# Retention and FFN on one core: the tails' block moved ahead of the last batch, FFN units regrouped so that w_out loads in long runs

## The chip, the cores and the metric

The kernel runs on one core of a Trainium2 chip. A core has a matrix engine (TensorE, PE in the profile, with its weight loads as PEld), VectorE (DVE), ScalarE (ACT), GpSimd (POOL) and SyncE (SP), which here only issues transfers. Data come from HBM into SBUF (128 partitions) through 16 DMA engines; matmul results go to PSUM, in banks of 128 x 512 fp32. The metric is the device time of one execution in microseconds. The kernel before takes 301.15 us, the median of 3 runs (301.05 to 301.19).

## The reference

Eight batches of 576 positions, eight heads of 64. Scores get a decay per head and a causal mask, there is no softmax; the result of all heads, side by side, is the input of an FFN with an ELU.

```python
scores = scale * np.matmul(q, k.transpose(0, 1, 3, 2))
Dmat = np.where(rel >= 0, gamma[:, None, None] ** rel[None, :, :], 0.0)
ret = scores * Dmat[None, :, :, :]
attn_out = np.matmul(ret, v)                      # [8, 8, 576, 64]
x = attn_out.transpose(0, 2, 1, 3).reshape(4608, 512)
h = x @ w_in                                      # w_in  [512, 2048]
g = np.where(h > 0.0, h, np.exp(np.minimum(h, 0.0)) - 1.0)
out = g @ w_out                                   # w_out [2048, 512], out [4608, 512] fp32
```

The order of the 2048 hidden units does not matter for the result, as long as the columns of w_in and the rows of w_out are taken in the same order.

## The kernel before

**Attention.** The 576 positions of a batch are two stretches of 256 and a tail of 64. An "item" is one stretch of one batch for four heads: q, k and v are loaded by SP, scaled by the decay factors into `qkn` (mostly on GpSimd), transposed (`qkT`; on TensorE for the first seven items, `turn_pe`, by a DMA transposition later), and matmuls then form scores, a state per 64 positions and the output. The tails of four batches make one item each, `t0` and `t1`; they come last in `ORDER`, and their operands lie in the tile `aside`. `put_x` copies the results into `xt`, the transposed FFN input.

**FFN.** Rows go in blocks. Blocks 0 to 5 are narrow (256 rows of the first three batches); 6, 8, 10, 12 and 14 are wide (512 rows of batches 3 to 7); "T" is wide too and holds the 512 tail rows. `ffn1` makes, for 128 hidden units (`ft`) at a time, four accumulating matmuls with weights from `w_in_sb` and `xt` moving; then ACT takes the exponential (L1145), ACT or VectorE the maximum with 0 (L1153, L1155), VectorE subtracts 1 and takes the minimum into `g` (L1160). For a wide block one unit fills a PSUM bank, for a narrow block two do. `ffn2` makes 128 output rows: 16 accumulating matmuls with `g` as weights and `w_out_sb[:, ft]` moving, then a copy to `ot` (L1200) and a store by SP (L1208). `rows_of` says which rows a tile of 128 stores: one transfer of 128 rows for batch rows, two of 64 for tails and for the tiles named in `HALVED`. The last 128 rows of all are cut by columns at `LAST`, 256, 128 and 128.

**Weights.** `w_in_sb` is [128, 4, 2048] and `w_out_sb` [128, 16, 512], both bf16; GpSimd's queue loads and converts them, four transfers each (L471, L479), issued between 9.2 and 20.1 us. The partition p of `w_out_sb[:, ft]` has to hold the row of w_out for the hidden unit that FFN1 left in partition p of the unit group `ft`.

**Order.** Nothing is ordered by hand. Every step is an `Op` with costs per engine, dependencies and a rank; `Plan.run` plays them through and gives each engine a fixed order, which is kept in the program. `seq` is the order of the FFN blocks, "T" put in `TAILS` places from its end; `base` and the ranks follow from it. DMA transfers have assumed durations, for w_out `dma=(2.62, 32, PIECE)`, which the change leaves alone. SP issues in its fixed order too, so that a store which waits for its copy holds up the loads and transpositions behind it.

**The places that matter below.** Item 4 is the first whose loads wait (`HOLD`, a small GpSimd memset at 20.66 us) until w_in is on its way; its q, k and v are issued at 20.82, 21.23 and 21.78 us, while w_in and w_out are still moving. Its q and k are scaled on GpSimd (L494) and transposed on TensorE (L558). At the end of the program stand the last copies and stores of the last FFN2 tile.

Of the kernel before, what the change touches and what calls it, by code (L numbers as in the profile page):

```python
# [17 lines left out]
P = 128  # L18
# [18 lines left out]
class Plan:  # L37
# [6 lines left out]
    def add(self, *a, **kw):  # L44
        op = Op(*a, **kw)
        self.ops.append(op)
        for key in op.use:
            self.users.setdefault(key, []).append(op)
            op.turn += self.owner.get(key, [])
        for cls, key, *_ in op.take:  # L50
            self.owner[key] = [op]
            if cls not in FREE and key not in LONE:
                op.turn += self.takers.get(cls, [])
                self.takers[cls] = [op]
        return op
# [147 lines left out]
TOGETHER = 1  # L203
EARLY = 5
LOOSE = True
TAILS = 0
NARROW = 3
SPREAD = 0
POOL0 = 3.6
# [9 lines left out]
AWAY = {}  # L219
TWO = False  # L220
LAST = (0, 256, 384, 512)
HALVED = ((12, 1),)
ORDER = (0, 1, 2, 3, 4, 5, 6, 7, "t0", "t1")
PE_TURN = 7
WG = ("ck11", "ck11", "ck11", "ck12")
# [16 lines left out]
def kernel(  # L242
# [18 lines left out]
    KJ = DM // P  # L261
# [13 lines left out]
    def mm(*a, **kw):  # L275
        return pin(nc.tensor.matmul(*a, **kw))  # L276
# [66 lines left out]
    w_in_sb = const.tile([P, KJ, DF], BF16, name="w_in_sb")  # L343
# [10 lines left out]
    def T(cls, key, shape, dt):  # L354
        return (cls, key, shape, dt)
# [20 lines left out]
    seq = [*range(2 * NARROW), *range(2 * NARROW, 2 * B, 2)]  # L376
    seq.insert(len(seq) - TAILS, "T")
    place = {blk: i for i, blk in enumerate(seq)}
# [6 lines left out]
    def xt_of(blk):  # L385
        return "xt", blk if blk == "T" else blk // 2
# [90 lines left out]
    def load_w_out(n, after):  # L477
        def emit(op):
            pin(nc.gpsimd.dma_start(w_out_sb[:, 4 * n : 4 * n + 4],  # L479
                                    moe_w_out[n * 512 : (n + 1) * 512, :].rearrange("(f p) n -> p f n", p=P)))  # L480

        w_out_ld[n] = add(f"wo{n}", {"POOL": 0.8}, [], emit, -1000, dma=(2.62, 32, PIECE), after=after)

# [479 lines left out]
    def by_block(key):  # L963
        return tiles[key].rearrange("p k n -> p (k n)").rearrange("p (t k n) -> p t k n", k=KJ, n=P)
# [156 lines left out]
    def ffn1(blk, p, rank):  # L1121
        hkey, ekey, gkey = ("h", blk, p), ("e", blk, p), ("g", blk, p)
        wide, xkey = width[blk] > TB, xt_of(blk)
        at0 = 0 if wide else blk % 2 * TB

        def emit(op):
            ph, xt = tiles[hkey], tiles[xkey]
            for f in range(1 if wide else 2):
                ft = p if wide else 2 * p + f
                for j in range(KJ):  # L1130
                    if blk == "T":
                        o, x = ph, xt[:, j]
                    else:
                        x = by_block(xkey)[:, at0 // P : (2 * TB if wide else at0 + TB) // P, j]
                        o = ph if wide else ph[:, f * TB : (f + 1) * TB]
                        o = o.rearrange("p (t n) -> p t n", n=P)
                    mm(o, w_in_sb[:, j, ft * P : (ft + 1) * P], x, start=(j == 0), stop=(j == KJ - 1))

        f1 = add(f"F1_{blk}_{p}", {"PE": 0.864 if wide else 0.873}, [*xdone[blk], w_in_ld[p // 4 if wide else p // 2]],
                 emit, rank, take=[T("f", hkey, [P, 512], FP32)], use=[xkey],  # L1140
                 after=None if LOOSE and place[blk] < 2 else chain.get(1))
        chain[1] = f1

        def emit_e(op):
            pin(nc.scalar.activation(tiles[ekey], tiles[hkey], AF.Exp))  # L1145

        ex = add(f"ex_{blk}_{p}", {"ACT": 0.6}, [f1], emit_e, rank, take=[T("e", ekey, [P, 512], FP32)],
                 use=[hkey], banks=[(hkey, 0)])

        def emit_m(op):  # L1150
            ph = tiles[hkey]
            if op.eng == "ACT":
                pin(nc.scalar.activation(ph, ph, AF.Relu))  # L1153
            else:
                pin(nc.vector.tensor_scalar_max(ph, ph, 0.0))  # L1155

        md = add(f"md_{blk}_{p}", {"ACT": 0.6, "DVE": 0.66}, [ex], emit_m, rank, use=[hkey], banks=[(hkey, 0)])

        def emit_g(op):
            pin(nc.vector.scalar_tensor_tensor(tiles[gkey], tiles[ekey], -1.0, tiles[hkey], ALU.add, ALU.min))  # L1160

        gdone[blk, p] = add(f"g_{blk}_{p}", {"DVE": 0.69}, [md], emit_g, rank, take=[T("g", gkey, [P, 512], BF16)],
                            use=[hkey, ekey], banks=[(hkey, 0)])

    def rows_of(blk, it):
        if blk == "T":
            return [(j * ST, ST, (2 * it + j) * S + FT * P) for j in range(2)]
        row = blk // 2 * S + blk % 2 * TB + it * P
        if (blk, it) in HALVED:
            return [(0, ST, row), (ST, ST, row + ST)]  # L1170
# [161 lines left out]
    for op in order:  # L1332
# [8 lines left out]
        if op.eng == "PE":  # L1341
            gap = op.start - last if op.start < 50 and op.take else 0.0
            if gap > 0:
                spot = tiles[op.take[0][1]]
                for n in range(int(gap * 0.8 / (0.107 if op.start < 7.0 else 0.056))):
                    if op.name.startswith("T"):
                        pin(nc.tensor.transpose(spot[:, n % 4], zero[:, :P], ident))
                    else:
                        mm((spot if len(spot.shape) == 2 else spot[:, 0])[:, :P], zero[:, :P], zero[:, :P],
                           start=True, stop=True)  # L1350
# [35 lines left out]
```

## Time and profile before

| | |
|---|---|
| median of 3 runs | 301.15 us (301.05 to 301.19) |
| the profiled execution | 300.55 us, of which the span from first to last instruction 298.8 us |
| TensorE's first matmul of the FFN / last matmul of all | 18.3 us / 294.0 us |
| weight loads of w_in / of g | 768 / 608, mean 98 ns each |
| narrow FFN1 matmuls (128 x 256) / wide (128 x 512) | 384 / 384 |
| FFN2 matmuls, 512 / 256 / 128 columns | 560 / 16 / 32 |
| issue to landing, median: w_in, w_out (512 KB each) | 9.2 us, 16.2 us |
| longest waits of TensorE by the profile | 1.3 us (start), 0.4 us, 0.3 us, 0.2 us |
| last matmul to end of span | 4.8 us |

A matmul's duration in the profile overlaps the next one's, since they are pipelined; the pace is read from the distance of starts. In the tables of groups a line gives engine, operation, output and inputs by name, shapes and the count, then busy time and the mean duration. In a timeline the first two numbers are start and duration in us, and the bracket at the end names what the engine waited for and how long. DMA lines name a queue: q0 is GpSimd's, q1 is SP's. A queue's share counts the time of its packets, and packets overlap, so that it can pass 100%.

### The profile page before, as it was taken

What the parts mean: (1) busy time and instruction counts of PE and PEld (TensorE: products, weight loads), DVE (VectorE), ACT (ScalarE), POOL (GpSimd) and SP (SyncE); (2) the same over time, 40 slices, a digit from 0 to 9 for tenths busy, and PEclk for the clock granted to TensorE, in tenths of its full rate; (3) what the DMA queues carried; (4) which work ended last, traced back from release to release, by engine and by line L of the source; (5) the groups of instructions that cost most, each with busy time, mean ns of one, the idle gap of its engine ahead of it and who ended that gap; (6) DMA issues with size and microseconds to landing.
All of it is one profiled execution on the core that took longest, in us unless ns stands there. A gap on an engine that the chain in (4) does not pass through costs nothing.

```text
span 298.8 us, 8957 instructions
## 1 busy us (share of the span) xinstructions
PE 291.7 (98%) x3589; PEld 166.1 (56%) x3589; DVE 175.2 (59%) x315; ACT 199.4 (67%) x391; POOL 136.3 (46%) x257
## 2 busy tenths in 40 slices
PE   7999999999999999999999999999999999999993
PEld 4788656767676754554545454545454544444443
DVE  5989935937765848788656465748353543343200
ACT  2459725858867758769787777787767677767421
POOL 5970379956767655758435546555223000000000
PEclk9999999999999999999999999999999999999999
DMA  7999998998899999999998999976694010110033
GB/s 208 271 207 213 222 289 199 197 194 184 181 204 209 175 217 206 205 182 230 255 249 234 204 176 241 189 168 147 151 162 122 29 37 35 52 56 36 35 72 70
DMA packets 141978, 50.14 MB, mean 168 GB/s; under 512 B 120688, under 2 KB 137456, under 8 KB 141936
## 3 DMA queue, kind: packets, MB, share of 16 engines
q1 hardware_dynamic: 137712, 45.37, 71.5%
q0 software_dynamic: 4224, 4.19, 8.4%
q8 instruction: 28, 0.46, 0.7%
q14 instruction: 14, 0.11, 0.1%
HBM read 36.70 MB, written 9.44 MB: 154 GB/s over the span
## 4 chain that ended last, share of the span: by engine, by line
PE 90%; DMA 3%; DVE 2%; POOL 2%; SPq 0%; issue 0%; ACT 0%; ACTq 0%; DVEq 0%
PE f L276 88%; PE sc L276 2%; DMA rv<-in_v_dram 2%; DMA qkT<-qkn 2%; POOL qkn L494 1%; DVE pt L937 1%; PE f L558 1%; POOL w_in_sb L471 0%; DVE qkn L494 0%; SPq L422 0%; DVE s_mid L834 0%; POOL s_mid L820 0%; POOL vn L545 0%; POOL s_end L820 0%; DVE end L812 0%
## 5 line engine op out<-in xcount | busy, mean ns | idle before, releaser
L1160 DVE SCALAR_TENSOR_TENSOR g<-e,f 128x512 bf16<-128x512 f32 x144 | 96.7, 685 | 86.4 <-ACT f L1153 70.9
L276 PE MATMUL f<-w_out_sb,g 128*128 128x512 bf16 (+2 forms) x608 | 143.3, 368 | 0.0
L276 PE MATMUL f<-xt,w_in_sb 128*128 128x256 bf16 (+1 forms) x768 | 140.9, 326 | 0.0
L1145 ACT ACTIVATE e<-f 128x512 f32<-128x512 f32 x144 | 84.9, 598 | 39.9 <-PE f L276 32.5
L276 PEld LDWEIGHTS <-w_in_sb 128*128 128x128 bf16 x768 | 74.5, 98 | 53.0
L276 PEld LDWEIGHTS <-g 128*128 128x128 bf16 x608 | 56.7, 98 | 58.3
L1153 ACT ACTIVATE f<-f 128x512 f32<-128x512 f32 x123 | 72.6, 592 | 0.0
L494 POOL TENSOR_TENSOR qkn<-rqk,far_q 128x256 bf16<-128x256 f32 x48 | 28.9, 616 | 9.3 <-DMA rqk<-in_q_dram 8.8
L494 POOL TENSOR_TENSOR qkn<-rqk,far_k 128x256 bf16<-128x256 f32 x48 | 29.1, 618 | 8.1 <-DMA rqk<-in_k_dram 7.6
L545 POOL CAST vn<-rv 128x512 bf16<-128x512 f32 x28 | 17.1, 612 | 21.6 <-DMA rv<-in_v_dram 18.8
L1200 ACT COPY ot<-f 128x512 f32<-128x512 f32 (+2 forms) x30 | 16.8, 561 | 11.1 <-PE f L276 11.0
L877 POOL CAST y<-mid 64x256 bf16<-64x256 f32 x36 | 14.2, 400 | 20.4 <-DVE mid L862 9.2
L972 ACT CAST xt<-f 128x512 bf16<-128x512 f32 x23 | 12.4, 589 | 15.9 <-PE f L276 15.9
L931 DVE TENSOR_TENSOR pt<-sc,mask_t 128x1024 bf16<-128x1024 f32 x12 | 14.6, 1218 | 2.4 <-PE sc L276 2.4
L1155 DVE TENSOR_SCALAR f<-f 128x512 f32<-128x512 f32 x21 | 14.6, 693 | 0.9 <-ACT e L1145 0.7
L618 POOL TENSOR_TENSOR aside<-aside,gq 128x256 bf16<-128x256 f32 x16 | 9.4, 615 | 11.6 <-DMA aside<-in_k_dram 11.4
L877 ACT CAST y<-mid 64x256 bf16<-64x256 f32 x31 | 11.9, 401 | 2.3 <-DVE mid L860 1.0
L494 POOL TENSOR_TENSOR qkn<-rqk,gq 128x256 bf16<-128x256 f32 x13 | 8.1, 633 | 11.5 <-DMA rqk<-in_q_dram 11.5
L862 DVE TENSOR_TENSOR mid<-f,mid 128x256 f32<-128x256 f32 x24 | 10.2, 424 | 2.7 <-PE f L276 0.5
L276 PE MATMUL f<-pt,vn 64*64 64x64 bf16 (+1 forms) x512 | 11.6, 202 | 0.1
L993 ACT CAST xt<-f 128x256 bf16<-128x256 f32 x10 | 4.2, 451 | 10.8 <-PE f L276 10.8
L937 DVE TENSOR_TENSOR pt<-sc,mask 128x1024 bf16<-128x1024 f32 x8 | 9.8, 1221 | 2.3 <-PE sc L276 2.2
(93 smaller groups left out, 173.8 us busy)
## 6 DMA issues: line engine op xcount, KB each, us to landing
rqk<-in_q_dram SPq DMA_DIRECT2D x48, 128.0 KB, 3.5
rqk<-in_k_dram SPq DMA_DIRECT2D x48, 128.0 KB, 3.3
rv<-in_v_dram SPq DMA_DIRECT2D x48, 128.0 KB, 3.7
out_dram<-ot SPq DMA_DIRECT2D x23, 256.0 KB, 2.8
rqk<-in_q_dram SPq DMA_DIRECT2D x8, 256.0 KB, 5.8
rqk<-in_k_dram SPq DMA_DIRECT2D x8, 256.0 KB, 5.4
rv<-in_v_dram SPq DMA_DIRECT2D x8, 256.0 KB, 5.6
w_in_sb<-in_moe_w_in_dram POOLq DMA_DIRECT2D x4, 512.0 KB, 9.2
```

What stands on the lines that cost most here:

```text
L276: return pin(nc.tensor.matmul(*a, **kw))
L494: pin(alu[op.eng].tensor_tensor(dst, tiles[raw][:, :, e], g, ALU.mult))
L545: pin(copy[op.eng](tiles["vn", n], tiles["rv", n]))
L877: pin(copy[op.eng](dst, tiles[key][j * D : (j + 1) * D]))
L931: pin(nc.vector.tensor_tensor(tiles[it.pt].rearrange("p i h n -> p (i h n)")[:, : 2 * w * C].rearrange("p (i x n) -> p i x n", i=2, n=C), ...
L937: pin(nc.vector.tensor_tensor(tiles["pt", n].rearrange("p i h n -> p (i h) n"), tiles[it.sc].rearrange("p i (h n) -> p (i h) n", h=2), mas ...
L972: pin(copy[op.eng](by_block(it.xt)[:, 2 * it.T + c], tiles[xkey, c].rearrange("p (h n) -> p h n", n=P)))
L1145: pin(nc.scalar.activation(tiles[ekey], tiles[hkey], AF.Exp))
L1153: pin(nc.scalar.activation(ph, ph, AF.Relu))
L1155: pin(nc.vector.tensor_scalar_max(ph, ph, 0.0))
L1160: pin(nc.vector.scalar_tensor_tensor(tiles[gkey], tiles[ekey], -1.0, tiles[hkey], ALU.add, ALU.min))
L1200: pin(copy[op.eng](tiles[okey][:, :cols], tiles[pkey][:, :cols]))
```

## The change

Three things are changed. (1) The tails' block moves from the last place of `seq` to the last but one, so that block 14 (batch 7) is computed last. (2) Instead of one tile, five tiles are stored in two halves: the last of block 10 and all four of block 12. (3) Of each 512 rows of w_out, partition p now holds rows 4p to 4p + 3 (one run of 2048 numbers in HBM and in SBUF) instead of rows p, 128 + p, 256 + p and 384 + p (four runs of 512). To match, the 128 hidden units of group `ft` become every fourth one of their 512, so FFN1's weight loads read every fourth column of `w_in_sb`, 8 bytes apart, where they read 128 neighbours. The number of instructions on TensorE, GpSimd, ACT and VectorE together stays; SP issues two transfers more.

```diff
-TAILS = 0
+TAILS = 1
...
-HALVED = ((12, 1),)
+HALVED = ((10, 3), (12, 0), (12, 1), (12, 2), (12, 3))
...
-                                    moe_w_out[n * 512 : (n + 1) * 512, :].rearrange("(f p) n -> p f n", p=P)))
+                                    moe_w_out[n * 512 : (n + 1) * 512, :].rearrange("(p f) n -> p f n", p=P)))
...
-                    mm(o, w_in_sb[:, j, ft * P : (ft + 1) * P], x, start=(j == 0), stop=(j == KJ - 1))
+                    mm(o, w_in_sb[:, j, ft // 4 * 512 + ft % 4 : (ft // 4 + 1) * 512 : 4], x, start=(j == 0), stop=(j == KJ - 1))
```

In the built program TensorE's order is the same for its first 5610 of 7180 instructions, which is up to the attention stretch that runs at 201.3 us before. Later the two differ in the order of the blocks. Before, the FFN1 groups of block 14 alternate with FFN2 groups of block 12, those of T with FFN2 of 14, and FFN2 of T stands alone at the end. After, FFN2 of block 12 runs in one piece around the tails' attention, then come the sixteen FFN1 groups of T in one piece, then FFN1 of 14 alternates with FFN2 of T, and FFN2 of 14 stands alone at the end.

## The prediction

> **What bounds the kernel now.** I read the busy table first, then the chain of waits, then the timeline of TensorE, because the first only says who is busy.
>
> ```profile
> span 298.8 us, 8957 instructions
> PE 291.7 (98%) x3589; PEld 166.1 (56%) x3589; DVE 175.2 (59%) x315; ACT 199.4 (67%) x391; POOL 136.3 (46%) x257
> PE 90%; DMA 3%; DVE 2%; POOL 2%; SPq 0%; issue 0%; ACT 0%; ACTq 0%; DVEq 0%
> 20.93 10.65 PE L276 MATMUL f<-xt,w_in_sb 128*128 128x256 bf16 x96
> 31.42 0.39 PE L558 MATMUL f<-ident,qkn 128*128 128x128 bf16 x4
> ```
>
> The last two lines (TensorE timeline, start and duration in us) are 96 FFN1 matmuls of a narrow block from 20.93 to 31.42: 10.49 / 96 = 109 ns each, with no wait between. Wide ones take 16 in 3.45 us (the output copies at 287.22 and 290.68 stand one tile of 16 apart), 216 ns each. FFN1 and FFN2 at these paces are 384 x 0.109 + (384 + 560) x 0.216 + 16 x 0.109 + 32 x 0.056 = 249 us of the 277 us from 17.2 to 294.2 (0.056: the last two 128-column tiles, whose copies start 0.89 us apart for 16 matmuls). Attention is the rest. So TensorE is the bound from 17 us on, its order is fixed in the program, and the change leaves it no matmul fewer. What can move the time: a new wait on TensorE, weight loads that no longer hide, and the 4.6 us behind its last matmul.
>
> **The change part by part: w_out.** Each of four loads copies 512 rows. The diff turns four runs of 512 numbers per partition into one of 2048 (the built copy has the form 128x2048 for 128x4x512). Here is what the DMA queues did from 20 to 24 us (first line) and from 25 to 36 us (the two others): packets, MB written, share of 16 engines.
>
> ```profile
> q0 software_dynamic: 829, 0.82, 123.8%
> ...
> q0 software_dynamic: 1589, 1.58, 84.3%
> q1 hardware_dynamic: 1593, 0.79, 35.5%
> ```
>
> q0 carries w_in and w_out, q1 everything that SP issues. Alone, q0 moved a packet of 1 KB every 4000 / 829 = 4.83 ns. Beside q1 the two alternate, 1589 packets against 1593, a pair every 11000 / 1589 = 6.92 ns, though q1's hold half the bytes. So a q1 packet costs 2.09 ns, and the share goes by packets. The loads of q, k and v for item 4 (SP, from 20.82 us) sit in that stretch: 256 KB in packets of 512 B, 512 packets each, 512 x 6.92 = 3.5 us a load, from about 24.4 us.
>
> If a run of 2048 numbers becomes one packet, w_out is 512 packets of 4 KB. No row has such a pair. At q0's own rate per byte it takes 4 x 4.83 + 2.09 = 21.4 ns, and the first q1 load of 512 packets needs 11.0 us where it needed 3.5: its landing moves by 7.4 us. Bounds: if 4 KB went at the 292 GB/s that both queues reach together from 36 to 40 us, 14.0 + 2.1 = 16.1 ns a pair, 8.3 us, 4.7 us later; by the instruction queue's row (28 packets, 0.46 MB, 0.7% of 16 engines: 1.2 us for 16.4 KB, so 0.6 us for the 8 KB read here, over 16 engines 37 ns) 39.5 ns, 20.2 us, 16.7 us later. I take 7.4, the row with the same bytes and the same cast. Who waits:
>
> ```profile
> 29.23 1.19 POOL L494 TENSOR_TENSOR qkn<-rqk,gq 128x256 bf16<-128x256 f32 x2 [8.43 <-DMA rqk<-in_q_dram]
> 31.31 0.32 PEld L558 LDWEIGHTS <-qkn 128*128 128x128 bf16 x4
> ...
> 32.85 1.19 POOL L494 TENSOR_TENSOR qkn<-rqk,gk 128x256 bf16<-128x256 f32 x2 [2.44 <-DMA rqk<-in_k_dram]
> ```
>
> POOL waits for item 4's q, scales it until 30.42, and TensorE transposes it at 31.42 (second transposition, k's: 34.68). The cover is 31.42 - 30.42 less some 0.1 to hand over, 0.9 us. The wait is then 7.4 - 0.9 = 6.5 us (bounds 3.8 and 15.8). Everything behind it on TensorE stands still, and it is not regained: POOL is in order too, item 4's state blocks stand ahead of item 5, so its busy stretch from 40 to 58 us shifts along. When q is through, w_out is through as well, and k and v follow at q1's own pace, inside the 3.3 us that TensorE takes from one transposition to the next. w_out itself lands earlier, for nothing: its first matmul at 33.4 us waits for no load now.
>
> By the Trainium skill (TensorE: Matmul & The Clock Gate, section Part 1) an idle stretch of some 3.4 us lets the matmul clock fall to half. The trace has the two paces, 423 ns for a 128x512 matmul in the first 4 us against 216 later, but no idle stretch after that to test it. By the page up to 2 us would come on top; the sum below leaves it out.
>
> **FFN1's columns.** 768 weight loads read every fourth column. None in the trace is strided. Contiguous ones take 98 ns each and keep up with a 56 ns pace in the last tiles, so a load has at least a factor of two before a narrow matmul's 109 ns shows it, four before a wide one's 216. Lower bound 0; upper, if four times 56 ns: 384 x (223 - 109) + 384 x (223 - 216) = 46 us. I take 0: the nearest row is the same load with the same bytes.
> By the Trainium skill (SBUF — State Buffer, the note on cachelines) a stride is free while two reads fall in a line of 16 bytes; 8 bytes between columns is just that, so by the page also 0. No run here shows it.
>
> **Tails' block before the last.** TensorE's instructions are the same up to some 200 us, then the same work in another order: the last 128-row tile is now whole rows of a batch, with one store where a tails' tile has two.
>
> ```profile
> 294.25 0.27 ACT L1200 COPY ot<-f 128x128 f32<-128x128 f32 x1 [0.63 <-PE f L276]
> 295.30 1.18 SPq L1208 DMA_DIRECT2D out_dram<-ot  x2
> out_dram<-ot SPq DMA_DIRECT2D x2, 64.0 KB, 2.0
> out_dram<-ot SPq DMA_DIRECT2D x4, 32.0 KB, 1.9
> ```
>
> The last copy ends at 294.52, but its two stores leave SP at 295.30 and 295.89, since four of some 0.6 us queue there. With one store a piece SP is free at 294.52, so the last leaves some 1.3 us earlier and lands in 2.0 us for 1.9. I take -1.3; bounds -0.6 (one issue less) and -1.8 (also the queue ahead of it).
> The price in front: sixteen wide FFN1 units of the tails now run back to back, 13.8 us. ACT then has 16 exponentials and about 10 relus at 0.49 us (two start 0.49 apart where it is full), 12.7 us; VectorE 16 products and 6 relus at 0.64, 14.1 us; six PSUM banks cover the 0.3. The run from 20.93 above was such a burst, and no matmul waited. Before it, the tails' two copies into xt (0.68 us, from 237.11 to 237.79) are covered by one FFN2 group, 0.86 us: 0 to 0.2, I take 0.1.
> The halved stores add issues on SP. Two pairs now stand before the last two transpositions of the tails, one waits for a copy at about 227 us; those transpositions then go at 228.5 and 229.8 instead of 225.1 and 226.5 and land 2.8 later, 232.6, for scores at 234.3. Cover 1.7 us, price 0.
>
> **Sum.** The profiled run took 300.55 us, 298.8 of it the span. 300.55 + 6.5 + 0.1 - 1.3 + 0 = 305.85. The median of the runs is 301.15, 0.6 more: 306.5.
>
> **Rivals.**
> (a) Faster: the software queue cuts the long runs, or the engines share otherwise, so q1 keeps its share and the wait at 31.42 never comes. It decides when q of item 4 lands less than 0.9 us later than now. Then only the end counts: 301.15 + 0.1 - 1.3 = 300.0. For it: all 4096 data packets of q0 have 1 KB, none shows that a longer one exists in that queue. Against it: the instruction queue has packets of 16 KB, the stores 2 KB, so the engines take what they are given.
> The Trainium skill (DMA: Bandwidth & Descriptors, section SWDGE vs HWDGE vs iDMA) lets a packet hold several descriptors up to about 4096 bytes; by that four short runs already went together and the share would not change, which is this rival. The trace's one-for-one alternation of 1 KB pieces differs.
> (b) Strided weight loads become the bound of the narrow blocks: it decides from 109 ns a load. At twice 56 ns, 112, they cost 384 x 3 ns = 1.1 us, at four times 46 us: with (a) 301 to 346. Against it: the hidden room above.
> (c) The long packets go but cut only in two (2 KB): the pair is 11.8 ns, q lands 2.5 us later and k 5.0, less its cover of 0.6: 4.4 us of wait, 304.4. It belongs to the forecast's side.
>
> **How the numbers follow.** Forecast with (c) 0.56, (a) 0.35, (b) 0.09. A measurement of this kernel tells about 0.2%, 0.6 us. Faster: (a) nearly whole, 0.35. Same: 0.03, a small wait and the shorter end cancelling. Slower: the forecast and (b), 0.62. The range reaches to (a) on one side, 300.0 less 0.5 = 299.5, and on the other to 309.5, a wait of 9.5 us, since the upper bound comes from another kind of transfer; left out are most of (b) and the top of the wait, some 0.12. The forecast's own range is 303.8 to 309.5.
>
> **What would show it.** Right: the DMA view shows some 512 packets above 2 KB on q0 and few q1 packets until 35 us; POOL's first scaling of item 4 starts near 36.7; TensorE has one wait of 4 to 8 us, before the transposition after the 96 narrow matmuls; narrow matmuls stay at 109 ns, and the last store leaves SP within 0.1 us of the last copy. Wrong: that scaling still at 29 to 30 us and no wait there, narrow matmuls above 110 ns, or a wait in the tails' burst.

## The result, and the profile after

The changed kernel takes 307.80 us, the median of 4 runs (307.59 to 308.30), where the kernel before takes 301.10 us (300.89 to 301.19). The ratio is 1.0226, 95% interval 1.0208 to 1.0244: slower by 6.7 us. The profiled execution took 308.30 us, 7.75 us more than that of before.

From the page of the changed kernel, its span, the busy table and the shares of the chain of waits:

```profile
span 306.6 us, 8945 instructions
...
PE 295.1 (96%) x3589; PEld 178.2 (58%) x3589; DVE 179.2 (58%) x323; ACT 195.3 (64%) x383; POOL 134.8 (44%) x257
...
PE 91%; DMA 4%; DVE 2%; POOL 1%; issue 0%; ACT 0%; POOLq 0%; ACTq 0%; DVEq 0%
```

TensorE still bounds the kernel, with the same 3589 matmuls. Its share fell from 98 to 96%, so there is a new wait, and its busy time grew by 3.4 us with no matmul more, so some matmuls became slower. TensorE's waits on the changed kernel (engine, line, what it waited for; us in total, times, longest) and its timeline from 18.5 us (start and duration in us; the wait before it in brackets):

```profile
PE f L276 <- DMA w_in_sb<-in_moe_w_in_dram: 6.8, 1, 6.8
PE f L276 <- DVE zero L281: 1.3, 1, 1.3
PE f L558 <- POOL qkn L494: 0.2, 1, 0.2
```

```profile
18.66 0.30 PE L276 MATMUL f<-xt,w_in_sb 128*128 128x256 bf16 x1
25.74 3.37 PE L276 MATMUL f<-xt,w_in_sb 128*128 128x256 bf16 x15 [6.78 <-DMA w_in_sb<-in_moe_w_in_dram]
...
30.35 10.99 PE L276 MATMUL f<-xt,w_in_sb 128*128 128x256 bf16 x96
41.18 0.39 PE L558 MATMUL f<-ident,qkn 128*128 128x128 bf16 x4
```

There is one long wait, but not where the prediction put it. It stands between the first and the second matmul of the whole FFN, and it is for w_in, not for item 4's q. Before, the same 16 matmuls ran without a break:

```profile
18.33 1.92 PE L276 MATMUL f<-xt,w_in_sb 128*128 128x256 bf16 x16
```

The transposition that was to wait (41.18) follows its 96 matmuls at once; it is 9.8 us late only because everything ahead of it is.

The windows of the wait, of the stretch after it and of the next ten microseconds on the changed kernel (stretch, length, then busy time and count of PE, PEld, DVE, ACT, POOL, then the granted clock, DMA share, GB/s):

```profile
18.70:25.70 7.00, 0.25 (x5) 0.06 (x1) 1.76 (x4) 0.00 (x0) 1.67 (x4) 0.65 1.20 212
25.70:31.00 5.30, 5.26 (x42) 3.82 (x43) 1.24 (x3) 2.62 (x5) 0.00 (x0) 0.50 1.06 217
31.00:41.00 10.00, 10.00 (x93) 9.98 (x92) 8.79 (x20) 9.05 (x20) 2.92 (x5) 1.00 1.05 270
```

After the idle 7 us TensorE works for 5.3 us at a granted clock of 0.50: the narrow FFN1 matmuls there start 213 ns apart, where 109 ns is their pace. From 31 us it is whole again. The 0.65 of the first row is a mean: the clock was whole until 20.8 us and 0.50 from there on, so it fell within the wait.

GpSimd's timeline on the changed kernel, and its DMA queues from 24 to 36 us (packets, MB, share of 16 engines):

```profile
36.03 1.19 POOL L494 TENSOR_TENSOR qkn<-rqk,gq 128x256 bf16<-128x256 f32 x2 [14.99 <-DMA rqk<-in_q_dram]
37.36 1.19 POOL L494 TENSOR_TENSOR qkn<-rqk,gk 128x256 bf16<-128x256 f32 x2
```

```profile
DMA packets 2167, 2.79 MB, mean 232 GB/s; under 512 B 107, under 2 KB 1691, under 8 KB 2165
...
q0 software_dynamic: 562, 1.96, 81.1%
q1 hardware_dynamic: 1603, 0.80, 25.4%
```

So w_out does go in long packets. While both queues had work, from 27 to 33 us, they moved 309 and 306 packets, one for one; most of q1's 1603 came after 33 us, when w_out was nearly through. In the whole run q0 has 2688 packets instead of 4224, 1536 fewer, which is 2048 packets of 1 KB become 512 of 4 KB. Item 4's q is scaled at 36.03 instead of 29.23 us, 6.8 us late, where 7.4 was forecast. But TensorE comes for it only at 41.18.

The end, from ACT's and SP's timeline and the list of DMA issues (KB each, median us to landing) of the changed kernel:

```profile
302.38 2.06 SPq L1208 DMA_DIRECT2D out_dram<-ot  x3
...
303.81 0.27 ACT L1200 COPY ot<-f 128x128 f32<-128x128 f32 x1 [0.63 <-PE f L276]
```

```profile
out_dram<-ot SPq DMA_DIRECT2D x2, 64.0 KB, 1.5
```

The last copy ends at 304.08 and the span at 306.56, 2.48 us later; before, the two were 294.52 and 298.83, 4.31 us apart. That is 1.8 us won: no store queues behind another, and the last lands in 1.5 us.

From these views the difference of the two profiled executions adds up. FFN1 starts 0.33 us later (18.66 for 18.33). The wait is 25.74 - 18.66 - 0.109 = 6.97. The transposition comes 41.18 - 31.42 = 9.76 us later in all, so the slow clock takes 9.76 - 0.33 - 6.97 = 2.46. A stall of TensorE of 0.55 us at 57.5 us before is one of 0.1 after: -0.45. The end: -1.8. Sum 7.5 of the 7.75 us; 0.2 were not traced.

**Why the second matmul waits for w_in.** This is TensorE's listing in the two built programs, the weight loads of FFN1 that wait for a w_in transfer (DMASW0 to DMASW3 are the four of them; the number ahead is the place on TensorE, and an instruction that only waits is put together with the one behind it):

```
before  629 L276 Ldweights w_in_sb [waits DMASW0_49]
        707 L276 Ldweights w_in_sb [waits DMASW1_49]
        803 L276 Ldweights w_in_sb [waits DMASW2_49]
        867 L276 Ldweights w_in_sb [waits DVE_49,DMASW3_49]
after   629 L276 Ldweights w_in_sb [waits DMASW0_49]
        631 L276 Ldweights w_in_sb [waits DMASW3_49,DMASW2_49,DMASW1_49]
```

Before, each quarter of w_in is waited for when its first unit comes. After, the second weight load waits for all four quarters, though its columns come from the first. The framework finds out which transfers a read depends on. A transfer of 512 columns fills four pieces per partition (one for each 128 rows of w_in, 2048 columns apart in the tile), so its first and last byte enclose parts of the other three. The first unit's columns with j = 0 lie ahead of the other transfers' first byte; those with j = 1 lie between first and last byte of all four. With 128 neighbouring columns the dependence was exact; with every fourth it behaves as if only the enclosing ranges were compared. That this is the rule inside the framework is inferred from the listing; that the wait comes of the strided read of one common tile is what e3 tests.

### The profile page after: what moved, and what is told of

Read it like the earlier page. It is cut to its first block, busy times and chain, and to the rows that moved or that the text cites. A ratio compares the mean times of both kernels' runs of the same rounds, so it can differ in the third digit from the quotient of the medians.

```text
span 306.6 us, 8945 instructions
## 1 busy us (share of the span) xinstructions
PE 295.1 (96%) x3589; PEld 178.2 (58%) x3589; DVE 179.2 (58%) x323; ACT 195.3 (64%) x383; POOL 134.8 (44%) x257
## 3 DMA queue, kind: packets, MB, share of 16 engines
q0 software_dynamic: 2688, 4.19, 7.5%
## 4 chain that ended last, share of the span: by engine, by line
PE 91%; DMA 4%; DVE 2%; POOL 1%; issue 0%; ACT 0%; POOLq 0%; ACTq 0%; DVEq 0%
PE f L276 88%; DMA w_in_sb<-in_moe_w_in_dram 3%; PE sc L276 2%; DMA rqk<-in_q_dram 1%; DVE pt L937 1%; PE f L558 1%; POOL qkn L494 0%; DVE qkn L494 0%; POOL w_in_sb L471 0%; DVE qkT L564 0%; DVE s_mid L834 0%; POOL s_mid L820 0%; POOL s_end L820 0%; DVE end L812 0%; PE f L1347 0%
## 5 line engine op out<-in xcount | busy, mean ns | idle before, releaser
L276 PE MATMUL f<-w_out_sb,g 128*128 128x512 bf16 (+2 forms) x608 | 141.1, 368 | 0.0
L276 PEld LDWEIGHTS <-w_in_sb 128*128 128x128 bf16 x768 | 85.8, 114 | 52.4 <-issue 7.1
L1153 ACT ACTIVATE f<-f 128x512 f32<-128x512 f32 x116 | 68.6, 594 | 0.0
L1155 DVE TENSOR_SCALAR f<-f 128x512 f32<-128x512 f32 x28 | 19.4, 694 | 0.9 <-ACT e L1145 0.7
L862 DVE TENSOR_TENSOR mid<-f,mid 128x256 f32<-128x256 f32 x24 | 10.2, 424 | 2.7 <-PE f L276 0.5
```

## The experiments

The theory after the result, A: the layout alone costs everything, by two delays that hide each other. The wait for all of w_in, with the slow clock behind it, sets the time; item 4's late q would cost about as much if that wait were gone. The rival B: the w_in wait is the only cost, and q's delay is harmless. It was open besides whether a part of the loss comes of the other order (the tails' burst, the stores).

**e1_tails_only**: the kernel before with the two constants of the tails, without the layout.

```diff
-TAILS = 0
+TAILS = 1
-HALVED = ((12, 1),)
+HALVED = ((10, 3), (12, 0), (12, 1), (12, 2), (12, 3))
```

> The kernel before with the tails' block last but one and the five halved tiles, both weight layouts as before. Theory (only the end of the program gains): 301.1 - 1.8 (last copy to end of span 4.3 us before, 2.5 after) + up to 0.1 = 299.4, no new wait on TensorE. Rival (the burst of sixteen FFN1 units of the tails, or the tails' copies into xt, cost something): above 300.2, with matmuls of that burst further apart than 216 ns.

Measured 299.23 us beside 301.12, ratio 0.9936 (0.9914 to 0.9957). TensorE's two longest waits by its table:

```profile
PE f L276 <- DVE zero L281: 1.3, 1, 1.3
PE f L558 <- POOL qkn L494: 0.7, 3, 0.3
```

No new wait. The span ends 2.5 us after the last copy (294.97 to 297.45) instead of 4.3. The order's part of the change is a gain of 1.9 us, which the end's 1.8 accounts for; nothing of the loss comes from there.

**e2_layout_only**: the changed kernel with the two constants as before.

```diff
-TAILS = 1
+TAILS = 0
-HALVED = ((10, 3), (12, 0), (12, 1), (12, 2), (12, 3))
+HALVED = ((12, 1),)
```

> The changed kernel with the tails' block last again and the one halved tile of before: only the weight layouts are new. Theory: the whole loss sits in the layout, 307.8 + 1.8 = 309.6, with one wait of some 7 us at 18.7 us. Rival (part of the loss comes with the order of the blocks): below 308.5.

Measured 309.08 us, ratio 1.0259 (1.0233 to 1.0284). The wait for w_in is 5.8 us here, behind one of 0.7 for ACT (`vn`). The layout costs 8.0 us, the order gives 1.9 back: 6.1, where the whole change costs 6.7; the intervals of the two ratios (each about 0.7 us either way) cover that gap.

**e3_tiles**: the changed kernel with w_in in four tiles, one for each transfer, so that a strided read can touch only its own.

```diff
-w_in_sb = const.tile([P, KJ, DF], BF16, name="w_in_sb")
+w_in_sb = [const.tile([P, KJ, 512], BF16, name=f"w_in_sb{n}") for n in range(4)]
...
-pin(nc.gpsimd.dma_start(w_in_sb[:, :, c], moe_w_in[:, c].rearrange("(j p) n -> p j n", p=P)))
+pin(nc.gpsimd.dma_start(w_in_sb[n0], moe_w_in[:, c].rearrange("(j p) n -> p j n", p=P)))
...
-mm(o, w_in_sb[:, j, ft // 4 * 512 + ft % 4 : (ft // 4 + 1) * 512 : 4], x, ...)
+mm(o, w_in_sb[ft // 4][:, j, ft % 4 : 512 : 4], x, ...)
```

> The changed kernel with w_in in four tiles of 512 columns instead of one, so that a strided weight load can only wait for the transfer of its own 512. Theory A (two delays, one hiding the other: the wait for all four w_in transfers, and item 4's q arriving late behind w_out's 4 KB packets): the wait at 18.7 us is gone, q is scaled near 36.0 as in the changed kernel, TensorE waits some 6 us before the transposition at 31.4 us, and its clock falls for some 2 us more: 306 to 307. Theory B (the long packets harm nothing, the w_in wait is the whole loss): no wait, 299.4.

Measured 305.41 us, ratio 1.0142 (1.0116 to 1.0168). TensorE's waits, GpSimd's timeline and TensorE's:

```profile
PE f L558 <- POOL qkn L494: 5.4, 3, 5.1
PE f L276 <- DVE zero L281: 1.3, 1, 1.3
```

```profile
36.12 1.18 POOL L494 TENSOR_TENSOR qkn<-rqk,gq 128x256 bf16<-128x256 f32 x2 [15.29 <-DMA rqk<-in_q_dram]
```

```profile
36.80 0.40 PE L558 MATMUL f<-ident,qkn 128*128 128x128 bf16 x2 [5.06 <-POOL qkn L494]
37.36 0.39 PE L558 MATMUL f<-ident,qkn 128*128 128x128 bf16 x2 [0.17 <-POOL qkn L494]
37.55 3.62 PE L276 MATMUL f<-xt,w_in_sb 128*128 128x256 bf16 x16
```

The w_in wait is gone, from the trace and from the listing: the four quarters of w_in are waited for at the places 629, 707, 803 and 867 again, as before the change, though the reads stay strided. In its place stands the wait that the prediction described: for q, before the transposition behind the 96 narrow matmuls, 5.1 us. The 16 matmuls after it take 3.62 us, some 213 ns each: the clock has fallen here too. A holds, B falls. The two transpositions of the first half start at 36.80, 0.7 us after the scaling began, so TensorE needs only the first of the two scalings. (The profiled execution is the longest of the four, 306.46 us.)

**e4_tiles_pad**: e3 and, besides, 16 unused numbers behind each row of w_out in SBUF, so that a run there is 512 numbers again. The strided reads stay.

```diff
-w_out_sb = const.tile([P, NFT, DM], BF16, name="w_out_sb")
+w_out_sb = const.tile([P, NFT, DM + 16], BF16, name="w_out_sb")
...
-pin(nc.gpsimd.dma_start(w_out_sb[:, 4 * n : 4 * n + 4],
+pin(nc.gpsimd.dma_start(w_out_sb[:, 4 * n : 4 * n + 4, :DM],
```

> As the kernel with four w_in tiles, and w_out_sb with 16 unused columns behind each row of 512, so that a partition's four rows are four runs again and w_out moves in packets of 1 KB; FFN1's weight loads stay strided. Theory A: neither delay, q scaled at 29.2, no wait above 0.6 us, 299.4; the strided loads, 113 ns for 98, hide behind matmuls of 109 ns because they overlap. Theory B: 299.4 too, and the same as the kernel with four w_in tiles. Rival (strided loads cost): 301 or more, narrow matmuls further apart than 109 ns.

Measured 299.79 us, ratio 0.9951 (0.9932 to 0.9970). GpSimd's and TensorE's timelines:

```profile
29.75 1.19 POOL L494 TENSOR_TENSOR qkn<-rqk,gq 128x256 bf16<-128x256 f32 x2 [8.44 <-DMA rqk<-in_q_dram]
```

```profile
32.05 0.39 PE L558 MATMUL f<-ident,qkn 128*128 128x128 bf16 x4
```

q is back (29.75) and TensorE waits for neither. From 24 to 36 us q0 and q1 move 1776 and 1588 packets, as before (1743 and 1667). With both waits gone the changed layout costs nothing that can be measured against e1 (the intervals overlap), although all 768 strided weight loads remain. The late q alone costs what lies between e4 and e3: 5.6 us.

**e5_pad**: the changed kernel with the padding alone, w_in in one tile as it was.

> The changed kernel (one w_in tile, strided loads) with 16 unused columns behind each row of w_out_sb, so that w_out moves in packets of 1 KB again. Theory A (the w_in wait alone makes the loss seen; the late q is hidden behind it): q scaled at 29.2, but the wait at 18.7 us of about 7 us and the slow clock after it stay, 307.8. Rival (the long packets hold up the last w_in transfer or lengthen the wait): below 306.5.

Measured 307.89 us, ratio 1.0223 (1.0197 to 1.0248). TensorE's and GpSimd's timelines:

```profile
25.40 3.20 PE L276 MATMUL f<-xt,w_in_sb 128*128 128x256 bf16 x15 [6.63 <-DMA w_in_sb<-in_moe_w_in_dram]
```

```profile
28.86 1.19 POOL L494 TENSOR_TENSOR qkn<-rqk,gq 128x256 bf16<-128x256 f32 x2 [7.96 <-DMA rqk<-in_q_dram]
```

q is early and the time is that of the changed kernel. So in the changed kernel the wait for w_in carries the whole loss, and the late q is entirely hidden behind it. (The profiled execution, 306.62 us, is the shortest of the four. In it the clock is whole again at 28.3 us, after 2.9 us of work at 0.50, where the changed kernel's profile has 5.3.)

**e6_fill**: the changed kernel with 132 matmuls of zeros (128 columns) before the first FFN1 unit, so that TensorE has work while w_in lands. They leave the result alone.

```diff
+for _ in range(132):
+    mm(ph[:, :P], zero[:, :P], zero[:, :P], start=True, stop=True)
```

> The changed kernel with 132 matmuls of zeros by zeros (128 columns, 56 ns each, 7.4 us) ahead of the first FFN1 unit, into the bank that this unit then starts afresh, so that TensorE is busy while it would wait for w_in. Theory (of the loss, some 2 us is the halved matmul pace after the wait, 18 matmuls at 213 ns for 109): the first FFN1 matmuls go at 109 ns and the time is 307.8 - 2.0 = 305.8; item 4's transposition still waits for nothing. Rival (the slow pace comes from elsewhere, for example from the strided loads or the moving transfers): unchanged, 307.8.

Measured 306.01 us, ratio 1.0167 (1.0149 to 1.0185). TensorE's timeline:

```profile
19.02 7.54 PE L277 MATMUL f<-zero 128*128 128x128 bf16 x132
26.40 1.91 PE L277 MATMUL f<-xt,w_in_sb 128*128 128x256 bf16 x16
...
28.98 10.67 PE L277 MATMUL f<-xt,w_in_sb 128*128 128x256 bf16 x96
```

The 16 matmuls take 1.91 us at once, as before. FFN1 goes on 0.8 us later than in the changed kernel (its second matmul at 26.51 for 25.74), and the run is still 1.8 us shorter. So the fallen clock is worth 1.8 us by the medians, 2.6 from the same start; the changed kernel's trace gave 2.46.

**e7_pad_two**: e3 with w_out in packets of 2 KB, two rows together and then 16 unused numbers.

```diff
-w_out_sb = const.tile([P, NFT, DM], BF16, name="w_out_sb")
+w_out_sb = const.tile([P, NFT // 2, 2 * DM + 16], BF16, name="w_out_sb")
...
-pin(nc.gpsimd.dma_start(w_out_sb[:, 4 * n : 4 * n + 4],
-                        moe_w_out[n * 512 : (n + 1) * 512, :].rearrange("(p f) n -> p f n", p=P)))
+pin(nc.gpsimd.dma_start(w_out_sb[:, 2 * n : 2 * n + 2, : 2 * DM],
+                        moe_w_out[n * 512 : (n + 1) * 512, :].rearrange("(p a f) n -> p a (f n)", p=P, a=2)))
```

> As the kernel with four w_in tiles, with w_out in packets of 2 KB (two rows of a partition in a run, 16 unused columns after them). Theory (SP's loads get one packet for each packet of w_out): 1024 packets of 2 KB, a pair every 11 to 12 ns, q of item 4 scaled some 2.5 us later than before, near 31.8, k some 4.5 to 5 us later, near 37.6; TensorE waits little for q and some 3 to 4 us for k, 303 to 304. Rival (what counts is only the bytes ahead in the queue): q scaled at 29.2 as with 1 KB, 299.4, or at 36.0 as with 4 KB, 305.4.

Measured 302.02 us, ratio 1.0043 (1.0022 to 1.0064). GpSimd's and TensorE's timelines:

```profile
31.45 1.18 POOL L494 TENSOR_TENSOR qkn<-rqk,gq 128x256 bf16<-128x256 f32 x2 [10.73 <-DMA rqk<-in_q_dram]
36.99 1.18 POOL L494 TENSOR_TENSOR qkn<-rqk,gk 128x256 bf16<-128x256 f32 x2 [4.37 <-DMA rqk<-in_k_dram]
```

```profile
37.66 0.28 PE L558 MATMUL f<-ident,qkn 128*128 128x128 bf16 x2 [1.65 <-POOL qkn L494]
```

The delay follows the packet's size: q is scaled at 29.75 with 1 KB (e4), 31.45 with 2 KB, 36.12 with 4 KB (e3). From 27 to 33 us, while both queues had work, q0 and q1 moved 869 and 867 packets in e4, 537 and 535 in e7, 313 and 312 in e3: one for one with every size, a pair every 6.9, 11.2 and 19.2 ns. So the rival, that only the bytes ahead count, falls. The time lies between the two, though below the 303 to 304 expected: the waits add up to 2.7 us (0.51, 0.29, 1.65, 0.28), no slow clock follows them in the profiled execution, and the stall at 57.5 us is gone here as well.

**e8_tails_plain**: e1 with no tile stored in halves.

```diff
-HALVED = ((10, 3), (12, 0), (12, 1), (12, 2), (12, 3))
+HALVED = ()
```

> The kernel before with only the tails' block last but one, and no halved tile at all. Theory (the halved stores are hidden): 299.2, the same as with five halved tiles, within 0.3. Rival (the halves matter, by keeping SP's waits for copies or the end in step): 0.6 or more above 299.2.

Measured 299.71 us, ratio 0.9958 (0.9936 to 0.9980). The median is 0.5 us above e1's, more than the 0.3 expected and less than the rival's 0.6, and the intervals of the two overlap. It can't be told from e1; the gain is that of the order, and what the halved stores do stays below what these runs resolve.

**e9_pace**: e4 with 384 further matmuls of zeros before the first FFN1 unit, whose weights are 128 neighbouring columns of w_in or every fourth. They only add time.

```diff
+for step in (1, 4, 1, 4):
+    for _ in range(64):
+        mm(ph[:, :P], w_in_sb[0][:, 0, : P * step : step], zero[:, :P], start=True, stop=True)
+for step in (1, 4):
+    for _ in range(64):
+        mm(ph[:, :64], w_in_sb[0][:, 0, : P * step : step], zero[:, :64], start=True, stop=True)
```

> The kernel with four w_in tiles and 1 KB packets, with 384 extra matmuls of zeros ahead of the first FFN1 unit, into its bank before it starts afresh: weights from w_in's first tile, in turns of 64 with neighbouring columns and 64 with every fourth, moving operands of 128 columns (two turns each) and then of 64 (one turn each). It measures whether a strided weight load has less room than the 109 ns of a narrow matmul. Theory (113 ns is how long a load takes, not how far apart two can be): 56 ns for both kinds at 128 columns, so there is at least half of the narrow matmul's time to spare; at 64 columns the first difference may show. Rival (strided loads cannot follow closer than some 100 ns): 56 ns for neighbouring columns and 100 or more for every fourth.

One execution was taken. TensorE's windows, for neighbouring and every fourth column at 128 moving columns, then for both at 64 (columns as above):

```profile
26.30:29.80 3.50, 3.50 (x66) 3.50 (x64) 0.00 (x0) 0.00 (x0) 0.00 (x0) 1.00 1.20 215
29.90:33.30 3.40, 3.40 (x65) 3.40 (x63) 0.00 (x0) 0.00 (x0) 1.19 (x2) 1.00 1.20 216
33.50:35.20 1.70, 1.70 (x64) 1.70 (x62) 0.00 (x0) 0.00 (x0) 1.19 (x2) 1.00 1.20 217
35.40:37.30 1.90, 1.90 (x63) 1.90 (x60) 0.00 (x0) 0.00 (x0) 0.12 (x1) 1.00 1.19 245
```

At 128 moving columns the starts stand 56 ns apart for both kinds. At 64 they stand 29 ns apart with neighbouring columns and 33 with every fourth. So a strided load keeps up with 33 ns, a third of a narrow matmul's 109.

Not tried: w_out issued later, behind item 4's loads, which would keep its long packets and might spare q.

## Why the prediction was right in size and wrong in place

The forecast was 306.5 us and slower; 307.80 was measured. That the size came out near is luck: the wait that set the time was another one, which the prediction did not have, and it happened to be about as long (7.0 us) as the one forecast (6.5).

- **The bound**, TensorE's paces: right, but while the granted clock was 0.50 (25.7 to 31.1 us) narrow matmuls started 213 ns apart. So the sign "narrow matmuls above 110 ns" did show, for a reason that the prediction had left out of its sum, see the clock below.
- **The strided weight loads, at 0: the step that failed.** The prediction asked how fast such a load is ("the nearest row is the same load with the same bytes") and not which transfers it waits for. The speed was right: in the changed kernel a load takes 114 ns instead of 98, the narrow pace stays at 109 (e4), and 33 ns still suffice (e9). So the stride is nearly free, not wholly: in e9's shortest matmuls the loads start 33 ns apart where neighbouring columns allow 29, and no FFN1 matmul of this kernel is short enough to show it. But the built program's listing already showed the second load waiting for all four w_in transfers, and nothing in the trace of before covers that: TensorE's FFN1 ran from 18.33 us without a break while w_in was still landing. That wait of 7.0 us, with the slow clock behind it, is the result (e5). What the prediction wanted to see, "one wait of 4 to 8 us, before the transposition after the 96 narrow matmuls", came with the size named, some 13 us ahead of the place named.
- **w_out's packets against q1**: right as a mechanism, by the count of packets (512 of 4 KB), by the dose (e4, e7, e3: q at 29.75, 31.45, 36.12) and by the place, once the wait ahead of it is taken away (e3). In size: q 6.8 us late for 7.4, the cover some 1.6 us instead of 0.9 because TensorE needs only the first of the two scalings (half of 1.19 us more), so a wait of 5.1 for 6.5. The term mis-sized is the pair of packets: 21.4 ns forecast, 19.2 measured in e3 (11.8 and 11.2 with 2 KB). In the changed kernel it cost nothing, since TensorE came 9.8 us late itself.
- **The clock**, left out of the sum: it belonged in. By the Trainium skill (TensorE: Matmul & The Clock Gate, section Part 1) an idle window of about 3.4 us halves the clock and about 3.4 us of work restore it. The traces agree in kind: waits that the profile lists at 6.8 us (changed kernel), 6.6 (e5), 5.8 (e2) and 5.1 (e3) halved it, while one of 1.7 us did not in e7's profile. The work done at 0.50 after the wait was not of one length: 5.3 us in the changed kernel and 5.4 in e3, but 3.4 in e2 and 2.9 in e5, so about 3.4 does not hold for each. Against the paces of before it cost 2.5 us in the changed kernel, 1.6 in e2 and 1.4 in e5, and by e6 1.8 to 2.6; the prediction's sentence had up to 2.
- **The end**, -1.3: 1.8 by the trace, 1.9 by e1; the last store leaves SP at 304.11, 0.03 us after the copy, and lands in 1.5 us where 2.0 was forecast, so the gain is at the outer bound.
- **The tails' burst and copies** at 0.1 and **the halved stores** at 0: no wait shows in either (e1, e8).
- **The rivals.** (a), q keeps its share: refuted by e3. The Trainium skill's rule behind it (DMA: Bandwidth & Descriptors, section SWDGE vs HWDGE vs iDMA: a packet, at whose end the engine may switch queues, holds up to 64 descriptors and preferably at most 4096 bytes) would have left the share alone if short runs filled such packets; here pieces of 1 KB and of 512 B move in equal numbers, and longer pieces take longer turns. (b), strided loads as the bound: refuted by e4 and e9. (c), 2 KB: not what happened, but its size was tested: q 1.7 to 2.2 us later for 2.5, and 2.7 us of wait for 4.4.

Summed with what was measured, the prediction's 300.55 becomes 300.55 + 0.3 + 7.0 + 2.5 - 0.5 - 1.8 = 308.05, against 308.30.

The best version is e1, the order without the layout: 1.9 us faster than before. With the new layout the best was e4, 299.79 us, which can't be told from e1.

## What to carry to other kernels

A read that becomes strided has two prices, its speed and what it is made to wait for: look in the built program's listing at each wait of the first instructions that read a tile filled by several transfers, and give each transfer its own tile if they have grown. Longer runs for one DMA queue are paid by the queue beside it when the two alternate by packets, so before lengthening them ask which transfer on the other queue is wanted next. And two delays in a row on one engine do not add: taking away only the one that shows uncovers the other, so the parts have to be undone singly and together.

## What the runs showed of the hardware

- The two queues moved equal numbers of packets while both had work, whatever the size: from 27 to 33 us q0 and q1 moved 869 and 870 packets with 1 KB (before), 537 and 535 with 2 KB (e7), 309 and 306 with 4 KB (after). With 4 KB, item 4's q was there 6.8 us later. (The counts do not tell single packets in turn from equal groups in turn.)
- The weight loads of every fourth bf16 column grew from 98 to 114 ns, by 16%, as the table of groups by form of the changed kernel shows (busy us, mean ns, idle before):

```profile
L276 PEld LDWEIGHTS <-w_in_sb 128*128 128x128 bf16 x768 | 85.8, 114 | 52.4 <-issue 7.1 <-DVE xt L988 0.4
```

  Yet they start as close as 33 ns apart (e9), against 29. A load's duration is no pace: several are under way at once.
- After an idle stretch of 5.1 to 7.0 us TensorE's pace was halved for 2.9 to 5.4 us of work, which cost 1.4 to 2.5 us on top of the wait (e5, changed kernel). The granted clock fell within the wait and stayed at 0.50 for 10.2 us in the changed kernel (20.8 to 31.1), for 6.8 in e2 (21.6 to 28.4), e3 (35.4 to 42.3) and e5 (21.5 to 28.3): three times and twice 3.4 us. The less of that stretch the wait itself uses up, the more work runs slowly. Filling the wait with matmuls of zeros took the slow stretch away (e6).
